# Batches 1 to 7: U, V and z loads issued by ScalarE instead of SyncE, V one step later and split two steps on

## The chip, the cores and the metric

The kernel runs on one core of a Trainium2 chip. The metric is the device time of one execution in microseconds (us). The median of three runs of the kernel before is 2323.25 us (2319.2 to 2325.48).

A core has five engines with their own instruction queues: TensorE (PE, with PEld for its weight loads), VectorE (DVE), ScalarE (ACT), GpSimd (POOL) and SyncE (SP), which does no arithmetic and here only issues DMAs. An engine works its instructions off in order; between engines, semaphores tell what is done.

## The reference, cut to what matters

```python
# u, v: 8 x 2496 x 256, z: 8 x 2496 x 64, fp32
scores = (1.0 / S) * np.matmul(z, z.transpose(0, 2, 1))
attn = np.maximum(scores, 0.0) ** 2
x = u * np.matmul(attn, v)                  # 19968 tokens of 256
# top-1 mixture of 8 experts, 256 -> 1024 -> 256
logits = x @ w_gate
expert_idx = np.argmax(logits, axis=1)      # gate_w: its softmax probability
for e in range(8):
    xe = x[expert_idx == e]
    out[expert_idx == e] = gate_w * (np.maximum(xe @ w1[e], 0.0) @ w2[e])
```

## The kernel before

The first stage, up to about 1345 us of the profile, is the attention. It goes batch by batch (`b`, 8 of them), in each through five chunks of 512 queries (`c`, the last has 448), and in each chunk through ten pairs of key blocks (`kp`): 400 steps, `s` in the loop, with `j` the place in the chunk. The second stage gathers tokens by expert and runs the two expert layers; the change doesn't touch it, except that it follows.

A step does two things on PE. `weighted` multiplies the squared scores of this step with V: 12 matmuls into `acc` (lines 343 to 346). `scores` prepares a later step, three ahead (`LA`): PE multiplies z with z into `ps_s` (lines 306, 307), or turns a block of scores that an earlier chunk stored (line 278), or takes such a block that DMA transposes have turned (line 332, then lines 263 to 265). ACT takes `ps_s` out of PSUM (line 315 with line 316, or line 279), and DVE makes of it a high and a low part, `thi` and `tlo`. `ps_s` has two buffers, so PE can begin the scores of a step only when ACT has emptied the ones of two groups before.

The inputs are loaded in pieces:
- V of a batch in ten pieces of 256 KB, `vr`, with three buffers (`fetch_v`, line 134). `split_v` makes a high part on ACT (line 139) and a low part on DVE (line 140), in `vt`. The V of batch `b + 1` is loaded and split during the last chunk of batch `b`.
- z of a batch in five pieces `zr`, with two buffers (`fetch_z`, line 120), split by `split_z` on ACT (lines 126, 127) and DVE (lines 128, 129), one in each chunk.
- U of a chunk in one piece `u` of 512 KB, with one buffer (`fetch_u`, line 146); `gate_x` multiplies it with the finished `acc` on DVE (line 366) at the chunk's end.

All these loads are issued by SP. SP also issues the DMA transposes of stored scores (line 332, 12 in a batch), those of the chunk's output rows (line 390, four in a chunk, in `turn_rows`; ACT and DVE write their source `th` in lines 385 and 386) and the store of these rows (line 471). As SP works in order, a load is issued behind the transposes that stand ahead of it.

The order on every engine is made by a scheduler from the order in which the code asks for work. Work inside `pinned(...)` is put behind the last instruction that each engine has so far; a load outside of it may be put earlier, as soon as its buffer is free.

Of the kernel before, what the change touches and what calls it, by code (L numbers as in the profile page):

```python
# [47 lines left out]
def fused_kernel(ctx: ExitStack, tc: tile.TileContext, zt, ut, v, wg, wcat, out):  # L48
    nc = tc.nc
# [3 lines left out]
    NKP = NK // 2  # L53
# [55 lines left out]
    zraw, vraw, ztiles, vtiles, utiles = {}, {}, {}, {}, {}  # L109
    zfirst = []  # L110

    def fetch_z(b, c):
        w = P * 4
        if b == 0 and c < 2:
            if c == 0:
                zfirst.append(sb.tile([P, 2, QC], F32, name="x", tag="x"))
            zraw[b, c] = zfirst[0][:, c]
        else:
            zraw[b, c] = sb.tile([P, w], F32, name="zr", tag="zr", bufs=2)
        nc.sync.dma_start(zraw[b, c], zt[b, :, c * w:(c + 1) * w])  # L120

    def split_z(b, c):

# [7 lines left out]

    def fetch_v(b, kp):
        vraw[b, kp] = sb.tile([P, 2, D], F32, name="vr", bufs=3)
        nc.sync.dma_start(vraw[b, kp], v[b, :, 2 * kp:2 * kp + 2, :])

    def split_v(b, kp):
        vr = vraw.pop((b, kp))
# [5 lines left out]
    def fetch_u(b, c):  # L143
        q0, n = chunks[c]
        u = sb.tile([P, 2, QC], F32, name="u")
        nc.sync.dma_start(u[:, :, :n], ut[b, :, :, q0:q0 + n])
        utiles[b, c] = u


# [200 lines left out]
    def pinned(work):  # L350

        last = {}
        for i in nc.cur_bb.bb.instructions[-400:]:
            last[i.engine] = i
        with ExitStack() as behind:
            for i in last.values():
                behind.enter_context(tc.issue_after(i))
            work()
# [489 lines left out]
    plain = [loads[LP - q][-1] for q in range(LP + 1)]  # L848
    for s, (b, c, kp) in enumerate(steps):
        j = s % NKP  # L850
        if j == 2:
            fetch_u(b, c)
        if j == 0:
            accs[b, c] = [ps1.tile([P, QC], F32, name=f"acc{d}", tag="ps1") for d in range(2)]
        if s < NKP:
# [18 lines left out]
        weighted(b, c, kp, j == 0, j == NKP - 1, *ready.pop(s), accs[b, c])  # L874
        if c == NC_ - 1 and b + 1 < B:

            for i in ((0, 1) if j == 0 else (j + 1,) if j < NKP - 1 else ()):
                fetch_v(b + 1, order_of(b + 1, 0)[i])
            if j:
                pinned(lambda: split_v(b + 1, order_of(b + 1, 0)[j - 1]))  # L880
        if c == 0 and j == 0 and b:
            pinned(lambda: split_v(b, order_of(b, 0)[-1]))

        zb, zc = (b + 1, c - 1) if c else (b, NC_ - 1)
        if 0 < zb < B:
            if j == ZF[c > 0]:
                fetch_z(zb, zc)
            if j == ZS[c > 0]:
                pinned(lambda: split_z(zb, zc))

# [112 lines left out]
```

## Time and profile before

| | |
|---|---|
| median of 3 runs | 2323.25 us (2319.2 to 2325.48) |
| the profiled execution | 2324.7 us |
| its span in the trace | 2322.9 us |
| PE busy | 2278.9 us (98%) |
| PEld busy | 1925.6 us (83%) |
| DVE busy | 1632.0 us (70%) |
| ACT busy | 1465.3 us (63%) |
| POOL busy | 625.7 us (27%) |
| loads issued by SP | V 80 x 256 KB, z 40 x 256 KB, U 32 x 512 KB and 8 x 448 KB |

The profile comes from one execution. "Busy" leaves out register, semaphore and DMA-issuing instructions; those stand in the trace under the engine's name with a q (SPq, ACTq). The idle time before an instruction is put down to what released it. A row of the timeline has the start in us, the duration in us, the engine, the line, the operation, what it writes and reads, and in brackets the idle time of the engine before it and its releaser.

### The profile page before, as it was taken

The numbers are of one execution on the slowest core, as the hardware profiler recorded it, in microseconds if no ns is written. First come the engines' busy times: TensorE is split into PE (matmuls) and PEld (weight loads), VectorE is DVE, ScalarE is ACT, GpSimd is POOL, SyncE is SP. The second block draws the span as 40 slices with busy tenths as digits, with TensorE's granted clock in tenths as the row PEclk, the third lists the DMA queues.
The fourth block names the chain that finished last, engine by engine and source line by source line (L and its number), as shares of the span: only waits on it lengthen the run. The fifth ranks groups of instructions, "written<-read, shape, count | busy, mean of one in ns | idle before, by whom it ended". The sixth has DMA issues, their size and how long they took to land.

```text
span 2322.9 us, 33688 instructions
## 1 busy us (share of the span) xinstructions
PE 2278.9 (98%) x12320; PEld 1925.6 (83%) x12320; DVE 1632.0 (70%) x2909; ACT 1465.3 (63%) x1985; POOL 625.7 (27%) x626
## 2 busy tenths in 40 slices
PE   9999999999999999999999989899999999999998
PEld 7888888888888888888888877688888888888887
DVE  8868868878778778877878766455566656657554
ACT  8768668677677777767776654355465555546454
POOL 1011111112102102102111244543445435345322
PEclk9999999999999999999999999899999999999999
DMA  6556656657567367467375484654566646457620
GB/s 163 104 92 135 97 86 135 93 95 134 85 105 132 80 116 121 79 118 125 79 114 95 121 176 89 189 123 131 154 152 173 176 128 207 134 146 194 151 89 29
DMA packets 454366, 287.31 MB, mean 124 GB/s; under 512 B 389100, under 2 KB 411130, under 8 KB 444976
## 3 DMA queue, kind: packets, MB, share of 16 engines
q1 hardware_dynamic: 422800, 165.98, 40.0%
q0 software_dynamic: 31392, 119.10, 17.6%
q8 instruction: 98, 1.61, 0.4%
q14 instruction: 76, 0.62, 0.1%
HBM read 149.79 MB, written 43.43 MB: 83 GB/s over the span
## 4 chain that ended last, share of the span: by engine, by line
PE 85%; issue 4%; DMA 3%; ACT 3%; DVE 2%; POOL 1%; another core or an unknown queue 1%; SPq 0%; POOLq 0%; ACTq 0%
PE ph L776 16%; PE acc L343 13%; PE acc L346 13%; PE acc L345 13%; PE y L799 11%; PE y L802 6%; PE ps_s L306 4%; PE ps_s L307 4%; DMA vr<-in_v_dram 2%; PE ps_s L278 2%; PE pt L398 1%; POOL out_dram L815 1%; PE ps_s L312 1%; DMA rows<-xrows,laidx 1%
## 5 line engine op out<-in xcount | busy, mean ns | idle before, releaser
L346 PE MATMUL acc<-thi,t 128*128 128x512 f32 (+1 forms) x1600 | 614.3, 386 | 0.0
L343 PE MATMUL acc<-thi,t 128*128 128x512 f32 (+1 forms) x1600 | 608.0, 392 | 1.1 <-issue 0.7
L345 PE MATMUL acc<-tlo,t 128*128 128x512 f32 (+1 forms) x1520 | 586.0, 386 | 0.1
L781 DVE SCALAR_TENSOR_TENSOR t<-ph,t 128x512 fp32r<-128x512 f32 (+1 forms) x328 | 220.3, 675 | 238.1 <-ACT t L780 192.5
L776 PE MATMUL ph<-thi,t 128*128 128x512 f32 (+2 forms) x1248 | 379.3, 361 | 3.8 <-issue 2.1
L780 ACT ACTIVATE t<-ph 128x512 fp32r<-128x512 f32 (+1 forms) x328 | 191.9, 591 | 289.1 <-PE ph L776 210.4
L346 PEld LDWEIGHTS acc<-thi,t 128*128 128x128 f32 x1600 | 300.2, 188 | 55.3 <-DVE t L140 0.6
L343 PEld LDWEIGHTS acc<-thi,t 128*128 128x128 f32 x1600 | 299.5, 188 | 54.4 <-DVE x L366 1.2
L345 PEld LDWEIGHTS acc<-tlo,t 128*128 128x128 f32 x1520 | 285.6, 188 | 50.8 <-DVE tlo L319 0.7
L476 POOL DMA_INDIRECT lst<-toks,posi x160 | 197.0, 1231 | 468.2 <-DVE posi L468 425.8
L799 PE MATMUL y<-t,t 128*128 128x512 f32 x1062 | 306.3, 397 | 13.5 <-DVE t L734 6.4
L776 PEld LDWEIGHTS ph<-thi,t 128*128 128x128 f32 x1248 | 226.1, 189 | 32.9 <-issue 2.9
L799 PEld LDWEIGHTS y<-t,t 128*128 128x128 f32 x1062 | 191.5, 191 | 48.7 <-ACT t L780 7.8
L776 PE MATMUL ph<-tlo,t 128*128 128x512 f32 (+2 forms) x624 | 225.6, 362 | 0.7 <-issue 0.7
L815 POOL DMA_INDIRECT out_dram<-tf,lfidx x136 | 143.7, 1057 | 273.4 <-DVE tf L813 245.5
L802 PEld LDWEIGHTS y<-t,t 128*128 128x128 f32 x1062 | 175.8, 190 | 35.2 <-DVE t L781 5.7
L802 PE MATMUL y<-t,t 128*128 128x256 f32 x1062 | 185.0, 283 | 3.6 <-DVE t L781 3.6
L315 ACT ACTIVATE tf<-ps_s 128x1024 f32<-128x1024 f32 (+1 forms) x145 | 133.8, 923 | 85.3 <-PE ps_s L307 43.3
L307 PE MATMUL ps_s<-t,t 128*128 128x512 f32 (+1 forms) x480 | 178.9, 376 | 0.0
L380 POOL MEMSET rows<- 128x64 int32 x40 | 6.8, 172 | 581.7 <-DMA xrows<-rows 359.6
L317 DVE CAST thi<-tf 128x1024 fp32r<-128x1024 f32 (+1 forms) x145 | 90.9, 627 | 102.3 <-ACT tf L316 94.5
L711 POOL DMA_INDIRECT rows<-xrows,lfidx x136 | 138.9, 1021 | 50.2 <-issue 38.3
(252 smaller groups left out, 4050.2 us busy)
## 6 DMA issues: line engine op xcount, KB each, us to landing
vr<-in_v_dram SPq DMA_DIRECT2D x80, 256.0 KB
xrows<-rows SPq DMA_DIRECT2D x32, 544.0 KB
u<-in_ut_dram SPq DMA_DIRECT2D x32, 512.0 KB
zr<-in_zt_dram SPq DMA_DIRECT2D x38, 256.0 KB
u<-in_ut_dram SPq DMA_DIRECT2D x8, 448.0 KB
xrows<-rows SPq DMA_DIRECT2D x8, 408.0 KB
rows<-th SPq DMA_TRANSPOSE x160
lst<-toks,posi POOLq DMA_INDIRECT x160
```

The lines of the kernel that those rows point to most:

```text
L307: nc.tensor.matmul(ps[:, i, m:n], lhsT=hl_k, rhs=lh_q[:, m:n], start=False, stop=True)
L343: nc.tensor.matmul(acc[d][:, :n], lhsT=vh, rhs=hi[:, i, :n], start=first and i == 0, stop=False)
L345: nc.tensor.matmul(acc[d][:, :n], lhsT=vh, rhs=lo[:, i, :n], start=False, stop=False)
L346: nc.tensor.matmul(acc[d][:, :n], lhsT=vl, rhs=hi[:, i, :n], start=False, stop=last and i == 1)
L476: i = nc.gpsimd.indirect_dma_start(out=lst1, out_offset=bass.IndirectOffsetOnAxis(ap=posi[:m, j:j + 1], axis=0), in_=toks[:m, col + j:col ...
L711: nc.gpsimd.indirect_dma_start(out=xg[:, s, :], out_offset=None, in_=src, in_offset=bass.IndirectOffsetOnAxis(ap=lists[which]["idx"][:, s, ...
L776: nc.tensor.matmul(o, lhsT=w1[:, part, dd, fs], rhs=xx[:, dd, :n], start=p == 0, stop=p == 5)
L780: nc.scalar.activation(hh[:, :m], ph[:, :m], AF.Relu)
L781: nc.vector.scalar_tensor_tensor(hl[:, :m], ph[:, :m], 0.0, hh[:, :m].bitcast(F32), op0=ALU.max, op1=ALU.subtract)
L799: nc.tensor.matmul(y, lhsT=h[:, cs], rhs=w2[:, f % 2].rearrange("p i d -> p (i d)"), start=f == 0, stop=False)
L802: nc.tensor.matmul(y[:, 0:D], lhsT=h[:, cs], rhs=w2[:, f % 2, 0, :], start=False, stop=f == NF - 1)
L815: d = nc.gpsimd.indirect_dma_start(out=out, out_offset=bass.IndirectOffsetOnAxis(ap=lists[which]["idx"][:, s, t:t + 1], axis=0), in_=yo[:, ...
```

## The change

For batch 1 and later, the loads of z, V and U are issued by ACT instead of SP: 35 z, 70 V and 35 U loads, 140 of 160. Those of batch 0 stay on SP. All loads of U, of z from batch 1 on and of V from batch 1 on are now pinned, so they are issued at their place in the code and no earlier. U is asked for at step 3 of a chunk instead of step 2. In the last chunk of a batch, piece `j` of the next batch's V is asked for at step `j` (before: pieces 0 and 1 at step 0, piece `j + 1` at step `j`), and piece `j - 2` is split at step `j` (before: `j - 1`); the last two pieces are split in steps 0 and 1 of the next batch.

```diff
--- before.py
+++ after.py
@@ -109,6 +109,9 @@
     zraw, vraw, ztiles, vtiles, utiles = {}, {}, {}, {}, {}
     zfirst = []
 
+    def loads_of(b):
+        return nc.scalar if b else nc.sync
+
     def fetch_z(b, c):
         w = P * 4
         if b == 0 and c < 2:
@@ -117,7 +120,7 @@
             zraw[b, c] = zfirst[0][:, c]
         else:
             zraw[b, c] = sb.tile([P, w], F32, name="zr", tag="zr", bufs=2)
-        nc.sync.dma_start(zraw[b, c], zt[b, :, c * w:(c + 1) * w])
+        loads_of(b).dma_start(zraw[b, c], zt[b, :, c * w:(c + 1) * w])
 
     def split_z(b, c):
 
@@ -131,7 +134,7 @@
 
     def fetch_v(b, kp):
         vraw[b, kp] = sb.tile([P, 2, D], F32, name="vr", bufs=3)
-        nc.sync.dma_start(vraw[b, kp], v[b, :, 2 * kp:2 * kp + 2, :])
+        loads_of(b).dma_start(vraw[b, kp], v[b, :, 2 * kp:2 * kp + 2, :])
 
     def split_v(b, kp):
         vr = vraw.pop((b, kp))
@@ -143,7 +146,7 @@
     def fetch_u(b, c):
         q0, n = chunks[c]
         u = sb.tile([P, 2, QC], F32, name="u")
-        nc.sync.dma_start(u[:, :, :n], ut[b, :, :, q0:q0 + n])
+        loads_of(b).dma_start(u[:, :, :n], ut[b, :, :, q0:q0 + n])
         utiles[b, c] = u
 
 
@@ -848,8 +851,8 @@
     plain = [loads[LP - q][-1] for q in range(LP + 1)]
     for s, (b, c, kp) in enumerate(steps):
         j = s % NKP
-        if j == 2:
-            fetch_u(b, c)
+        if j == 3:
+            pinned(lambda: fetch_u(b, c))
         if j == 0:
             accs[b, c] = [ps1.tile([P, QC], F32, name=f"acc{d}", tag="ps1") for d in range(2)]
         if s < NKP:
@@ -874,17 +877,16 @@
         weighted(b, c, kp, j == 0, j == NKP - 1, *ready.pop(s), accs[b, c])
         if c == NC_ - 1 and b + 1 < B:
 
-            for i in ((0, 1) if j == 0 else (j + 1,) if j < NKP - 1 else ()):
-                fetch_v(b + 1, order_of(b + 1, 0)[i])
-            if j:
-                pinned(lambda: split_v(b + 1, order_of(b + 1, 0)[j - 1]))
-        if c == 0 and j == 0 and b:
-            pinned(lambda: split_v(b, order_of(b, 0)[-1]))
+            if j > 1:
+                pinned(lambda: split_v(b + 1, order_of(b + 1, 0)[j - 2]))
+            pinned(lambda: fetch_v(b + 1, order_of(b + 1, 0)[j]))
+        if c == 0 and j < 2 and b:
+            pinned(lambda: split_v(b, order_of(b, 0)[j - 2]))
 
         zb, zc = (b + 1, c - 1) if c else (b, NC_ - 1)
         if 0 < zb < B:
             if j == ZF[c > 0]:
-                fetch_z(zb, zc)
+                pinned(lambda: fetch_z(zb, zc))
             if j == ZS[c > 0]:
                 pinned(lambda: split_z(zb, zc))
 
```

In the built program, this is what the scheduler makes of it on ACT, at the beginning of the last chunk of batch 0, where the V of batch 1 comes in (`t` is the high part of V, `thi` the high part of scores, `th` the source of the row transposes). Before:

```order
L428 ACTIVATE ex<-dl 128x32
L279 CAST thi<-ps_s 128x2x448 x4
L139 CAST t_1593<-vr 128x512
L279 CAST thi<-ps_s 128x2x448
L139 CAST t_1625<-vr 128x512
L265 CAST thi<-tf 128x2x448
L139 CAST t_1678<-vr 128x512
L385 COPY th<-x 128x1024
L265 CAST thi<-tf 128x2x448
L139 CAST t_1709<-vr 128x512
```

The same place on ACT in the changed kernel, whose line numbers are three higher here (139 has become 142, 279 has become 282, 265 has become 268, 385 has become 388; V is loaded in line 137, z in line 123):

```order
L431 ACTIVATE ex<-dl 128x32
L282 CAST thi<-ps_s 128x2x448 x3
L137 DMA vr<-in_v_dram 128x512
L282 CAST thi<-ps_s 128x2x448
L137 DMA vr<-in_v_dram 128x512
L282 CAST thi<-ps_s 128x2x448
L142 CAST t_1616<-vr 128x512
L137 DMA vr<-in_v_dram 128x512
L123 DMA zr<-in_zt_dram 128x512
L268 CAST thi<-tf 128x2x448
L142 CAST t_1671<-vr 128x512
L268 CAST thi<-tf 128x2x448
```

Each split stands one instruction of score work later, and DMA issues now stand between ACT's instructions.

On SP, in the same chunk and the beginning of the next batch, before:

```order
L146 DMA u<-in_ut_dram 128x2x448
L134 DMA vr<-in_v_dram 128x512 x2
L390 DMA_TRANSPOSE rows<-th 128x4x128 x4
L134 DMA vr<-in_v_dram 128x512 x2
L120 DMA zr<-in_zt_dram 128x512
L134 DMA vr<-in_v_dram 128x512 x3
L332 DMA_TRANSPOSE s_1819<-th 128x16x128
L134 DMA vr<-in_v_dram 128x512
L146 DMA u<-in_ut_dram 128x2x512
L471 DMA xrows<-rows 128x4x272
```

And in the changed kernel (line 390 has become 393, 332 has become 335, 471 has become 474, 146 has become 149):

```order
L149 DMA u<-in_ut_dram 128x2x448
L393 DMA_TRANSPOSE rows<-th 128x4x128 x4
L335 DMA_TRANSPOSE s_1814<-th 128x16x128
L474 DMA xrows<-rows 128x4x272
L335 DMA_TRANSPOSE s_1814<-th 128x16x128
L335 DMA_TRANSPOSE s_1977<-th 128x16x128
```

The V and z loads are gone from between SP's transposes; the U load of batch 0 stays. From here on SP issues transposes and stores only.

## The prediction

> **What bounds the kernel now.** First come the two lines at the head of the page, for the span and the engines; then the table of busy time by stage.
>
> ```profile
> span 2322.9 us, 33688 instructions
> PE 2278.9 (98%) x12320; PEld 1925.6 (83%) x12320; DVE 1632.0 (70%) x2909; ACT 1465.3 (63%) x1985; POOL 625.7 (27%) x626
> ...
> core 0: us, PE busy (x) PEld busy (x) DVE busy (x) ACT busy (x) POOL busy (x), PEclk, DMA share, GB/s
> 0.00:100.00 100.00, 98.60 (x472) 76.84 (x473) 86.30 (x137) 81.63 (x92) 11.74 (x30) 1.00 0.61 140
> 100.00:1340.00 1240.00, 1236.30 (x6779) 1038.18 (x6778) 965.71 (x1680) 874.50 (x1003) 195.31 (x194) 1.00 0.60 107
> 1340.00:1420.00 80.00, 70.56 (x406) 59.09 (x404) 45.44 (x99) 39.34 (x56) 37.26 (x38) 1.00 0.81 158
> 1420.00:2227.00 807.00, 787.33 (x4198) 676.00 (x4197) 489.51 (x919) 429.16 (x762) 364.40 (x349) 0.99 0.58 155
> 2227.00:2322.00 95.00, 86.07 (x473) 75.46 (x471) 45.03 (x76) 40.66 (x75) 17.03 (x18) 0.97 0.10 35
> ```
>
> The reader is to see where PE has idle time at all. The loads that move belong to the stretch from about 100 to 1340 us, and there PE is busy 1236.30 of 1240.00 us: 3.70 us are idle. Busy alone doesn't say that PE runs at its pace, so I looked at single matmuls, in the timeline of PE where the trouble with V is largest.
>
> ```profile
> 850.21 0.36 PE L346 MATMUL acc<-thi,t 128*128 128x448 f32 x1
> ...
> 853.51 0.36 PE L346 MATMUL acc<-thi,t 128*128 128x448 f32 x1
> 854.21 0.50 PE L306 MATMUL ps_s<-t 128*128 128x512 f32 x1 [0.33 <-ACT tf L315]
> ...
> 858.71 0.36 PE L346 MATMUL acc<-thi,t 128*128 128x448 f32 x1
> 858.90 0.48 PE L306 MATMUL ps_s<-t,t 128*128 128x512 f32 x1
> ```
>
> From 850.21 to 853.51 us matmuls follow each other; the starts that the timeline gives are 0.20 us apart for 448 columns, with each lasting 0.36 us, so they overlap. One pause of 0.33 us stands there, and then the score group at 858.90 us starts on time. Next, all that PE waits for between 100 and 1330 us, from the view of the waits:
>
> ```profile
> PE ps_s L306 <- ACT tf L315: 2.8, 4, 1.3
> PE ps_s L278 <- DVE tlo L280: 0.8, 2, 0.7
> ```
>
> Six waits, 3.6 us in all. That is all that a change of loads in this stage can give back. The chain that ended last seems to say otherwise; it has four long pieces of V loads, at four of the seven places where a next batch's V comes in:
>
> ```profile
> 328.31 11.18 DMA vr<-in_v_dram
> 841.22 10.18 DMA vr<-in_v_dram
> 1013.46 10.68 DMA vr<-in_v_dram
> 1184.74 10.12 DMA vr<-in_v_dram
> ```
>
> They come to 42 us, but PE works through them, as its timeline shows; the chain only walks back along what ended last, and the load ended 0.33 us later than PE could hide. The 42 us are not there to be won.
>
> **What the V loads do now.** At one such boundary, ACT and SP:
>
> ```profile
> 845.89 0.95 ACT L316 ACTIVATE tf<-tf 128x896 f32<-128x896 f32 x1
> 851.43 0.62 ACT L139 CAST t<-vr 128x512 fp32r<-128x512 f32 x1 [4.58 <-DMA vr<-in_v_dram]
> ...
> 835.84 0.57 SPq L146 DMA_DIRECT2D u<-in_ut_dram  x1
> 841.22 2.79 SPq L134 DMA_DIRECT2D vr<-in_v_dram  x2
> 844.83 6.45 SPq L390 DMA_TRANSPOSE rows<-th  x4
> ```
>
> The fourth V piece is issued at 841.22 us behind U and lands about 10.2 us later; four row transposes are issued from 3.6 us after it, and their issue ends as it lands. ACT stands still for 4.58 us in front of the split, and PE loses 0.33 us through it. So a stall of 4.58 us on ACT costs PE almost nothing, since scores are three steps ahead.
>
> **The change part by part.** (a) The wait. With V on another queue and both its request and its split a step later, ACT should no longer stand before the fourth split. I take the whole first row of PE's waits as caused by it, since the pause at 854.21 us has this cause in the rows above and there are four of each: −2.8 us. Bounds: 0 (another V piece is late instead) and −3.7 us (all idle time of the stage).
>
> (b) The price on ACT. 140 issues move: 70 of V, 35 of z, 35 of U. No DMA is issued by ACT before, so the nearest rows are those of SP, together with its transposes:
>
> ```profile
> L134 SPq DMA_DIRECT2D vr<-in_v_dram x80: 327/336/1053, 1.3 to 1206.4; - x80
> L120 SPq DMA_DIRECT2D zr<-in_zt_dram x38: 327/714/1256, 2.7 to 1162.3; - x38
> L146 SPq DMA_DIRECT2D u<-in_ut_dram x40: 570/576/1053, 4.6 to 1356.2; - x40
> L332 SPq DMA_TRANSPOSE s<-th x96: 1317/2074/5038, 16.8 to 1333.8; - x96
> L390 SPq DMA_TRANSPOSE rows<-th x160: 1188/1259/9655, 61.9 to 1394.2; - x160
> ```
>
> By the medians: 70 x 0.336 + 35 x 0.714 + 35 x 0.576 = 68.7 us of ACT's sequencer, where ACT has 1240 − 874.5 = 365 us idle. What counts is whether the issue stops ACT's arithmetic. The sequencer runs ahead of it:
>
> ```profile
> L385 ACTq EVENT_SEMAPHORE  x2: 17/28/38, 841.6 to 841.6; - x2
> L385 ACT COPY th<-x x1: 1042/1042/1042, 843.7 to 843.7; 128x1024 uint16<-128x1024 uint16 x1
> ```
>
> ACT's sequencer did the waits of line 385 at 841.6 us, 2.1 us before the copy itself began. An issue of 0.34 us in such a place is covered by what ACT has already queued. I take 0, by these nearest rows. The cover is thinnest from 840 to 875 us, where V is split:
>
> ```profile
> 840.00:875.00 35.00, 34.67 (x192) 29.95 (x190) 28.52 (x51) 28.30 (x36) 0.33 (x2) 1.00 0.79 144
> ```
>
> ACT is busy 28.30 of 35 us; 6.70 us are idle, 4.58 of them the wait above. And PE has some patience: the group at 858.90 us uses the buffer that ACT emptied with this instruction,
>
> ```profile
> 855.55 0.90 ACT L279 CAST thi<-ps_s 128x896 fp32r<-128x896 f32 x1
> ```
>
> ended at 856.45 us, so 2.45 us before PE wanted it. ACT can fall behind by about that much before PE stops. Without cover, the price is the second rival.
>
> (c) A new wait on ACT. A V load needs its buffer free, so it waits for DVE's low part of three pieces before (line 140), and behind it in ACT's queue stand the next emptying of scores and the next split, for which PE and DVE wait. In the timelines of ACT and DVE:
>
> ```profile
> 858.89 0.60 ACT L139 CAST t<-vr 128x512 fp32r<-128x512 f32 x1
> 862.22 0.68 DVE L140 TENSOR_TENSOR t<-vr,t 128x512 fp32r<-128x512 f32 x1
> ```
>
> DVE ended 3.41 us after ACT's cast did. The load that waits for it stands a step later than this split. A step is 3.43 us: a batch has 50, and two V pieces of the chain, at 841.22 and 1013.46 us, are 172.2 us apart. So the wait is over about when it is reached: 0, at most a few tenths, inside the 2.45 us.
>
> (d) U and z elsewhere, one each in a chunk: pinned, with a buffer that DVE has freed by then; ACT has its 365 us. U is asked for a step (3.4 us) later and wanted at the chunk's end, more than six steps on: 0. (e) SP is freed of 140 issues; nothing on PE waits for SP in this stage: 0. (f) In the expert stage only the moment at which it begins changes: 0, either way by what PE idles in the change-over from 1340 to 1420 us, which is the third rival.
>
> Sum: −2.8 us. The profiled execution took 2324.7 us, 1.8 more than its span and 1.45 more than the median; so 2321.9 us as against it, 2320.5 as against the median. I predict **2321 us**: no difference that a measurement can tell, since about 0.3%, or 7 us, is what one of this kernel can separate (2316.3 to 2330.2 us count as the same).
>
> **The rivals.** *It doesn't do what it should: V still comes late.* V goes to another queue, but to the same DMA engines, and in the new order the fourth piece is issued behind U on that queue again. If its 10.18 us stay, against two steps or 6.9 us until the split, ACT waits 3.3 us in place of 4.58, and PE has its 2.8 us of waits or some of them: 2324.7 us. For it speaks that the transposes, which began after the load, ended with it. The Trainium skill has the same, page DMA: Bandwidth & Descriptors, section Issuing engines are not separate DMA queues: all queues end on the same 16 DMA engines, and another issuing engine only saves the time of issuing. By that rule the total would be this rival's; one queue carried both here, so the trace can't yet tell the two apart.
>
> *ACT falls behind (slower).* Every issue shows on ACT and waits for SP's transposes too. In 840 to 875 us there are ten V, two z and two U: 3.4 + 1.4 + 1.2 = 6.0 us. SP's transposes take 96 x 2.07 + 160 x 1.26 = 400 us, 30% of the 1340; an issue that has to wait for one loses half of it, between 0.6 and 1.0 us, say 0.85, so 14 x 0.30 x 0.85 = 3.6 us. Of 9.6 us, ACT takes 6.7 − 4.58 = 2.1 if V still waits, PE's patience 2.45; 5.0 us reach PE, at seven boundaries 35 us: 2360 us. If V's wait is gone, 9.6 against 6.7 + 2.45 leaves 0.4 us a boundary. So it decides from 4.6 us of uncovered issue time per boundary, when V also still waits. Against it: the 2.1 us by which ACT's sequencer was ahead.
>
> The Trainium skill has a rule for this, page Perfetto Trace Analysis, section DMA Instruction — HWDGE (DVE, Sync): the hardware that makes the descriptors is shared by the engines that issue this way and locked for one of them at a time, and the waiting for the lock counts into the instruction. By it, ACT's issue rows would grow whenever SP is in a transpose. With one issuing engine, no row here shows it; without the rule the sum stays as it is.
>
> *The change-over gains (faster).* There SP's queue is slow, and PE pauses:
>
> ```profile
> 1362.44 16.49 SPq L390 DMA_TRANSPOSE rows<-th  x4
> ...
> 1381.73 0.50 PE L776 MATMUL ph<-thi,t 128*128 128x512 f32 x1 [0.97 <-DVE x L366]
> 1389.04 0.74 PE L802 MATMUL y<-t,t 128*128 128x256 f32 x4 [3.37 <-DVE t L781]
> 1401.18 0.40 PE L776 MATMUL ph<-thi,t 128*128 128x512 f32 x1 [1.63 <-issue]
> 1417.96 0.70 PE L799 MATMUL y<-t,t 128*128 128x512 f32 x2 [1.04 <-DVE tf L813]
> ```
>
> Four transposes took 16.49 us there instead of about 5, behind the last U load on SP's queue. If U's leaving shortens that, up to 0.97 + 3.37 + 1.63 + 1.04 = 7.0 us go, and with 3.7 of the attention the time is 2324.7 − 10.7 = 2314.0 us. Against it: gathers fill the same DMA engines then (DMA share 0.81), and U is still among them.
>
> **How the numbers follow.** My forecast 0.50; V still late 0.16; ACT behind 0.23; the change-over 0.11. The first two lie within 0.3%: same 0.66, slower 0.23, faster 0.11. The range goes from 2313 us (the third rival and a margin of 1) to 2342 us, half of the slower rival's 35 us above 2324.7; beyond it I leave what is left of that rival.
>
> **What would show it.** (a) right: no ACT wait for V at line 139's split above 1 us, and PE's first row of waits under 1 us; wrong: 3 us at another V piece. (b) right: ACTq rows near SP's medians and ACT's idle time before its next instruction unchanged; wrong: rows of 1 us and more, and PE waiting for line 315 or 279 between V splits. (c) wrong: ACTq issues held by line 140. If PE's idle time from 100 to 1340 us is over 10 us, the forecast is wrong in the place of the second rival; if it is under 4 and the time still moves by more than 7 us, the change-over or the expert stage did it, which I hold at 0.

## The result, and the profile after

The changed kernel takes 2353.44 us (median of 6 runs, 2345.03 to 2362.01) against 2323.64 us (median of 6 runs) for the kernel before: a ratio of 1.0129, 95% interval 1.0107 to 1.0151. It is 30 us slower; the prediction was 2321 us, in a range that ended at 2342 us. The profiled execution took 2351.25 us.

The head of the page, and the table of busy time by stage, of the changed kernel:

```profile
span 2349.5 us, 33649 instructions
PE 2289.4 (97%) x12320; PEld 1931.1 (82%) x12320; DVE 1634.1 (70%) x2909; ACT 1465.6 (62%) x1985; POOL 628.5 (27%) x626
```

```profile
100.00:1340.00 1240.00, 1221.27 (x6651) 1023.16 (x6650) 952.53 (x1654) 862.15 (x988) 190.67 (x185) 1.00 0.63 105
1340.00:1420.00 80.00, 71.30 (x413) 60.27 (x412) 48.01 (x89) 42.31 (x53) 28.31 (x29) 0.96 0.85 158
```

In the stretch from 100 to 1340 us PE was idle 3.70 us before; now it is 1240 − 1221.27 = 18.73 us. The last matmul into `acc` starts at 1408.4 us in place of 1378.1 us, so the attention carries the whole 30 us; the stage behind it takes no longer than before (from the first `ph` matmul to the end of the span 940.9 us, before 944.5).

The view of the waits (what waited, for what: us in total, times, longest). First the row of the kernel before for V, from 100 to 1340 us; then the changed kernel, four rows from 100 to 1340 us and the last one from 1340 to 1420 us:

```profile
ACT t L139 <- DMA vr<-in_v_dram: 27.7, 10, 5.6
```

```profile
ACT t L142 <- DMA vr<-in_v_dram: 40.0, 16, 6.4
ACT t L129 <- DMA zr<-in_zt_dram: 13.8, 8, 3.0
PE ps_s L281 <- ACT tf L318: 9.4, 4, 3.3
PE ps_s L309 <- ACT tf L318: 6.3, 4, 3.1
...
PE acc L346 <- ACT thi L282: 5.4, 1, 5.4
```

ACT's waits for V have not gone; they grew from 27.7 us (10 times) to 40.0 us (16 times), waits for z have come in, and PE, which lost 2.8 us to ACT, now loses 15.7 us there and 5.4 us more in the last chunk.

Which pieces of V are late is read at one boundary, from batch 3 to batch 4, in the timeline of the changed kernel (start, duration, engine, line; the idle time before it and its releaser in brackets):

```profile
678.14 0.96 POOL L479 DMA_INDIRECT lst<-toks,posi  x1 [26.67 <-DVE posi L471]
679.40 0.96 POOL L479 DMA_INDIRECT lst<-toks,posi  x1 [0.30 <-issue]
680.66 1.47 POOL L479 DMA_INDIRECT lst<-toks,posi  x1 [0.30 <-DMA xrows<-rows]
681.11 0.33 ACTq L137 DMA_DIRECT2D vr<-in_v_dram  x1
682.44 0.96 POOL L479 DMA_INDIRECT lst<-toks,posi  x1 [0.31 <-issue]
682.82 0.33 ACTq L137 DMA_DIRECT2D vr<-in_v_dram  x1
...
692.65 0.62 ACT L142 CAST t<-vr 128x512 fp32r<-128x512 f32 x1 [6.42 <-DMA vr<-in_v_dram]
693.03 1.11 ACTq L123 DMA_DIRECT2D zr<-in_zt_dram  x1
694.23 0.55 ACTq L149 DMA_DIRECT2D u<-in_ut_dram  x1
694.87 0.94 ACT L268 CAST thi<-tf 128x896 fp32r<-128x896 f32 x1 [1.61 <-DVE lw L405]
...
697.18 0.91 ACT L318 ACTIVATE tf<-ps_s 128x896 f32<-128x896 f32 x1
...
698.14 1.97 PE L281 MATMUL ps_s<-ident,s 128*128 128x128 f32 x8 [3.28 <-ACT tf L318]
```

The reader is to see that it is pieces 0 and 1 now, not the fourth. They are asked for at 681.11 and 682.82 us, in the midst of four scatters by which POOL writes token numbers into the list of an earlier chunk, 4 bytes each (`lst`, line 479). ACT reaches the split and stands 6.42 us; behind the split in its queue stands the emptying of `ps_s` (line 318), so PE runs out of scores and stands 3.28 us. Part of that is a second delay: behind the split ACT issues z and U, and the conversion of line 268 starts 0.09 us after the second issue ends, 1.61 us late. (The view names a reduction on DVE, but that had ended at 694.16 us.) In v_only, a run below in which ACT issues neither z nor U, the same conversion follows its split at this boundary without a pause:

```profile
688.90 0.62 ACT L142 CAST t<-vr 128x512 fp32r<-128x512 f32 x1 [7.05 <-DMA vr<-in_v_dram]
...
689.43 0.94 ACT L268 CAST thi<-tf 128x896 fp32r<-128x896 f32 x1
```

In the kernel before, the timeline of the boundary from batch 4 to 5 has these pieces far ahead:

```profile
695.62 3.45 SPq L134 DMA_DIRECT2D vr<-in_v_dram  x2
703.60 0.45 SPq L134 DMA_DIRECT2D vr<-in_v_dram  x1
...
838.21 0.96 POOL L476 DMA_INDIRECT lst<-toks,posi  x1 [0.30 <-issue]
...
839.37 0.63 ACT L139 CAST t<-vr 128x512 fp32r<-128x512 f32 x1
841.84 0.62 ACT L139 CAST t<-vr 128x512 fp32r<-128x512 f32 x1
843.20 0.61 ACT L139 CAST t<-vr 128x512 fp32r<-128x512 f32 x1
```

Pieces 0 to 2 of batch 5 were issued at 695 to 704 us, as soon as their three buffers were free, some 140 us ahead of their splits, and no split waited. Only the fourth piece, asked for at 841.22 us just behind the last scatter (838.21 us), was long there too.

The pauses cost PE twice. The table of busy time for four short stretches of the changed kernel, each behind a pause; the third number from the end is the granted TensorE clock:

```profile
350.00:353.40 3.40, 3.12 (x8) 2.62 (x9) 2.15 (x5) 2.63 (x5) 0.00 (x0) 0.51 1.23 209
524.00:527.40 3.40, 3.40 (x11) 3.04 (x10) 3.33 (x5) 3.32 (x6) 0.00 (x0) 0.50 1.09 161
698.10:701.50 3.40, 3.36 (x13) 3.19 (x14) 2.40 (x5) 3.33 (x5) 0.20 (x1) 0.50 1.10 344
1374.00:1380.80 6.80, 5.88 (x22) 5.14 (x23) 6.21 (x14) 2.31 (x4) 3.65 (x3) 0.50 0.79 248
```

For 17 us the clock is at half, which is worth at most 8.5 us of work; the attention before has no such stretch. So 15.0 us more idle time of PE up to 1340 us, 4.7 us more in the last chunk (6.4 in place of 1.6) and 8.5 us of clock make 28.2 of the 30.2 us.

### The profile page after: what moved, and what is told of

It is laid out like the page before. It is cut to its first block, busy times and chain, and to the rows that moved or that the text cites. A ratio compares the mean times of both kernels' runs of the same rounds, so it can differ in the third digit from the quotient of the medians.

```text
span 2349.5 us, 33649 instructions
## 1 busy us (share of the span) xinstructions
PE 2289.4 (97%) x12320; PEld 1931.1 (82%) x12320; DVE 1634.1 (70%) x2909; ACT 1465.6 (62%) x1985; POOL 628.5 (27%) x626
## 3 DMA queue, kind: packets, MB, share of 16 engines
q8 instruction: 98, 1.61, 0.4%
## 4 chain that ended last, share of the span: by engine, by line
PE 78%; DMA 8%; issue 5%; ACT 4%; DVE 3%; POOL 1%; another core or an unknown queue 1%; SPq 0%; ACTq 0%; POOLq 0%; DVEq 0%
PE ph L779 17%; PE acc L346 12%; PE acc L349 12%; PE y L802 11%; PE acc L348 11%; PE y L805 6%; PE ps_s L309 4%; DMA zr<-in_zt_dram 4%; PE ps_s L310 4%; DMA vr<-in_v_dram 3%; PE ps_s L281 1%; DMA s<-th 1%; PE pt L401 1%; ACT tf L318 1%
## 5 line engine op out<-in xcount | busy, mean ns | idle before, releaser
L479 POOL DMA_INDIRECT lst<-toks,posi x160 | 202.1, 1263 | 526.7 <-DVE posi L471 486.2
L318 ACT ACTIVATE tf<-ps_s 128x1024 f32<-128x1024 f32 (+1 forms) x145 | 133.5, 921 | 78.6 <-PE ps_s L310 41.4
L269 DVE TENSOR_TENSOR tlo<-tf,thi 128x1024 fp32r<-128x1024 f32 (+1 forms) x96 | 115.3, 1201 | 52.7 <-ACT thi L268 49.9
```

Of the source, the lines that this page charges most:

```text
L318: nc.scalar.activation(a[:, :, m:n], ps[:, :, m:n], AF.Relu)
L479: i = nc.gpsimd.indirect_dma_start(out=lst1, out_offset=bass.IndirectOffsetOnAxis(ap=posi[:m, j:j + 1], axis=0), in_=toks[:m, col + j:col ...
```

## The experiments

All times are ratios to the kernel before, run beside it. The first theory, A: V pieces 0 to 2 have lost their lead and now are loaded where loads are slow; ACT, in order, stands at the split, and PE behind it. B is the prediction's second rival, that ACT pays for the issues. C: the pinned places or the later split as such. `V waits` are the waits of ACT's splits for V from 100 to 1340 us, `PE idle` is 1240 us less PE's busy time there, and `attention` is how much later than in the kernel before (1378.1 us) the last matmul into `acc` starts. The three come from one profiled execution each.

| kernel | ratio (95%) | V waits, us | PE idle, us | attention, us |
|---|---|---|---|---|
| changed kernel | 1.0129 (1.0107 to 1.0151) | 40.0 | 18.7 | +30.2 |
| issue_price | 1.0025 (1.0008 to 1.0042) | 28.7 | 3.8 | +1.3 |
| v_early | 1.0123 (1.0091 to 1.0155) | 3.1 | 10.3 | +21.5 |
| scat_early | 1.0157 (1.0095 to 1.0219) | 53.6 | 10.2 | +47.1 |
| v_as_before | 1.0047 (1.0027 to 1.0067) | 32.8 | 6.1 | +10.2 |
| v_early0 | 1.0048 (1.0027 to 1.0068) | 2.5 | 7.6 | +21.3 |
| all_on_sp | 1.0022 (1.0002 to 1.0042) | 40.8 | 8.9 | +10.2 |
| engine_only | 1.0049 (1.0032 to 1.0066) | 24.6 | 12.8 | +14.5 |
| u_as_before | 1.0125 (1.0089 to 1.0162) | 51.2 | 24.9 | +31.1 |
| scat_late | 1.0141 (1.0098 to 1.0183) | 4.5 | 25.2 | +39.9 |
| v_early0_u | 1.0015 (0.9997 to 1.0034) | none | 2.3 | −1.4 |
| v_only | 1.0083 (1.0056 to 1.0111) | 50.9 | 19.6 | +22.5 |
| v_only_early0 | 0.9981 (0.9964 to 0.9998) | 12.0 | 1.0 | −3.1 |
| before_scat_late | 1.0255 (1.0238 to 1.0273) | 9.4 | 41.4 | +56.1 |

The ratio holds the second stage as well, which no edit here touches. In these profiles it took 933 to 951 us (944.5 in the kernel before), but for before_scat_late, which ran on a faster chip; why it varies isn't known. The last column is steadier: four kernels that were profiled twice differ in it by 1 to 5 us. Where ratio and column disagree, the column is the better sign of what the loads did.

Three numbers for each V load are worked out from the traces: its lead (from issue to split), the time from its issue to its last packet, and ACT's idle time just before the split. For batches 1 to 7, the medians (idle time: mean):

| kernel | piece 0: lead, load, idle | piece 1: lead, load, idle | piece 3: lead, load, idle |
|---|---|---|---|
| before | 143.0, 3.8, 0 | 142.4, 2.4, 0 | 10.1, 6.4, 3.5 |
| changed | 8.7, 7.9, 3.9 | 11.3, 10.3, 0.9 | 7.6, 5.9, 0 |
| v_early | 30.9, 6.5, 0 | 26.8, 4.2, 0 | 8.1, 7.7, 0.1 |
| v_early0 | 125.4, 5.3, 0 | 121.2, 3.7, 0 | 10.8, 9.8, 0.1 |
| all_on_sp | 9.4, 3.4, 0 | 10.7, 4.9, 0.2 | 9.3, 7.5, 2.0 |
| engine_only | 142.1, 3.3, 0 | 141.3, 2.3, 0.3 | 8.6, 6.3, 3.5 |
| scat_late | 5.0, 2.3, 0.5 | 4.9, 2.3, 0.2 | 6.7, 3.1, 0 |
| v_only | 10.4, 8.2, 5.8 | 12.2, 8.7, 1.3 | 6.9, 2.9, 0 |

### The price of the issues (issue_price)

```diff
+    def ping(b):
+        if b:
+            d = sb.tile([P, 4], F32, name="dm", bufs=8)
+            nc.scalar.dma_start(d[0:1], zt[b, 0:1, 0:4])
...
+        if j == 3:
+            pinned(lambda: ping(b))
...
+            pinned(lambda: ping(b + 1))
...
                 fetch_z(zb, zc)
+                pinned(lambda: ping(zb))
```

> The kernel before, with all loads left where they were, and 140 further DMAs of 16 bytes that ACT issues at the places where the changed kernel issues U, V and z (nothing reads them). Theory A (lead): the loss comes from V pieces 0 to 2 being asked for only some 7 us ahead of their split, not from issuing on ACT: the ratio to the kernel before lies within 0.997 and 1.003, PE's idle time from 100 to 1340 us stays under 6 us. Theory B (price of the issues on ACT, the recorded second rival): 20 to 30 us longer, ratio 1.009 to 1.013.

Measured: 1.0025. The added issues and the stretch of the attention, in the line view and in the table of busy time:

```profile
L115 ACTq DMA_DIRECT2D dm<-in_zt_dram x140: 208/209/757, 58.4 to 1360.0; - x140
```

```profile
100.00:1340.00 1240.00, 1236.25 (x6776) 1037.45 (x6775) 964.93 (x1678) 872.91 (x1004) 178.16 (x193) 1.00 0.59 106
```

140 issues of 209 ns leave PE's idle time at 3.75 us. By its interval the kernel is 2 to 10 us slower, so not quite nothing, but at most a third of the loss. The changed kernel's own V issues take 334 ns at the median and 506 at most:

```profile
L137 ACTq DMA_DIRECT2D vr<-in_v_dram x70: 334/334/506, 155.0 to 1233.7; - x70
```

Theory B is out as the main cause, but its mechanism is there in part. From 100 to 1340 us of the changed kernel ACT's arithmetic stands idle 14 times until an issue of its own ends, as at 694.87 us above; the issues fill 10.7 us of these pauses, 2.4 us in the longest. issue_price has no such pause, but its issues are shorter and nothing in it makes ACT wait for V first. v_only, below, has 1.7 us of such time in place of 10.7, and PE's idle time is as long.

### Thirty microseconds of lead (v_early)

```diff
-            pinned(lambda: fetch_v(b + 1, order_of(b + 1, 0)[j]))
+            if j > 2:
+                pinned(lambda: fetch_v(b + 1, order_of(b + 1, 0)[j]))
+        if c == NC_ - 2 and 4 <= j <= 6 and b + 1 < B:
+            pinned(lambda: fetch_v(b + 1, order_of(b + 1, 0)[j - 4]))
```

> The changed kernel, with the first three V pieces of a next batch asked for in steps 4 to 6 of the chunk before the last (about 30 us ahead of their split in place of 7), still by ACT and pinned; the number of issues on ACT and the splits stay. Theory A: the waits of ACT for V fall from 40 us to under 20, PE's idle time at the seven boundaries goes, what stays is the last chunk of batch 7 (about 7 to 10 us): 2328 to 2338 us, ratio 1.002 to 1.006. Theory B: nothing changes, 2350 us and more, ratio 1.011 to 1.015.

Measured: 1.0123, a miss in the time. The waits for V went (3.1 us), as theory A says, but others came. The view of the waits of v_early from 100 to 1340 us, and its timeline in the chunk before the last of batch 4:

```profile
ACT tf L266 <- DMA s<-th: 23.3, 7, 5.1
ACT t L129 <- DMA zr<-in_zt_dram: 18.4, 12, 3.7
...
ACT t L142 <- DMA vr<-in_v_dram: 3.1, 7, 1.2
```

```profile
822.89 8.40 SPq L335 DMA_TRANSPOSE s<-th  x2
...
823.75 0.34 ACTq L137 DMA_DIRECT2D vr<-in_v_dram  x1
827.75 0.33 ACTq L137 DMA_DIRECT2D vr<-in_v_dram  x1
...
834.23 1.36 ACT L266 COPY tf<-s 128x1024 uint16<-128x1024 uint16 x1 [5.05 <-DMA s<-th]
```

At the new place V meets the two score transposes whose result ACT needs first in the next chunk; they take 8.40 us, ACT stands 5.05 us in front of line 266, and PE pauses 2.76 us at 837 us. The V lead isn't enough; what else is under way at the time counts. In the profile the attention ends 21.5 us late in place of 30.2, and the second stage takes 950.6 us, which hides that gain in the total. The theory was mended: a load that ACT issues at its place meets other DMAs, and whichever of them has the nearest deadline stops ACT.

### Over a hundred microseconds of lead (v_early0)

The same edit with `if c == (b == 0) and 5 <= j <= 7` and piece `j - 5`: pieces 0 to 2 come in the batch's first chunk, in batch 0 in its second.

> The changed kernel, with the first three V pieces of a next batch asked for in steps 5 to 7 of the batch's first chunk (of its second in batch 0), by ACT and pinned; more than 100 us ahead of their split, as the kernel before had them, and away from the score transposes whose result is wanted at the beginning of the last chunk. Theory A, mended (crowding: a load that ACT issues at its place meets other DMAs on the same engines, and whichever of them has the nearest deadline stalls ACT; asked for 30 us ahead V met the score transposes of the chunk before the last): ACT waits for V under 10 us and no score transpose there takes over 4 us, so what stays is z and the last chunk of batch 7: 2330 to 2341 us, ratio 1.003 to 1.008. Theory C (the lead of V isn't the cause, pinning or the later split is): 2345 us and more, ratio over 1.010.

Measured: 1.0048, inside, though partly by luck: the attention ends 21.3 us late, no earlier than in v_early, and the second stage took 933.0 us in place of 950.6. What bears on theory A is the stretch up to 1340 us: V no longer stops ACT (2.5 us), no score transpose is waited for longer than 2.0 us, and PE idles 7.6 us in place of v_early's 10.3. The last chunk, in turn, has become slower. What stays, in the view of the waits (the first row from 100 to 1340 us, the others from 1335 to 1385 us):

```profile
ACT t L129 <- DMA zr<-in_zt_dram: 28.1, 13, 4.0
...
ACT tf L266 <- DMA s<-th: 15.0, 1, 15.0
PE acc L346 <- ACT thi L282: 11.3, 1, 11.3
```

### V alone, and all but V (v_only, v_as_before, v_only_early0)

v_only is the kernel before with only the V part of the change; v_as_before is the changed kernel with only that part put back; v_only_early0 is v_only with the edit of v_early0.

> The kernel before with the V part of the change alone: ACT, pinned, split two steps on; z and U as before on SP. Theory A: pieces 0 to 2 are asked for 6 to 12 us ahead, the boundaries cost 15 to 25 us, the last chunk of batch 7 nothing: 2335 to 2348 us, ratio 1.006 to 1.011. If V's new place costs only together with z and U on the same queue: 2328 us and less, ratio under 1.004.

> The changed kernel with V alone put back: SP, unpinned, split one step on. z and U stay on ACT, pinned, U at step 3. Theory A: the seven boundaries are as in the kernel before, the last chunk of batch 7 keeps its loss and ACT waits some us for z: 2326 to 2338 us, ratio 1.001 to 1.006. Theory B: half of the 140 issues stay, so half of the loss: 2338 to 2342 us, ratio about 1.0065.

> The V part of the change alone with its lead given back: ACT, pinned, split two steps on, pieces 0 to 2 asked for in steps 5 to 7 of the batch's first chunk; z and U as before on SP. It is what the prediction took the change to be. Theory A: no boundary loses, ACT waits for V under 5 us, PE idles under 6 us from 100 to 1340 us: 2315 to 2324 us, ratio 0.997 to 1.001. If the issues on ACT or the later split cost something of their own: ratio 1.003 and more.

Measured: 1.0083, 1.0047 and 0.9981, each inside theory A's range of times; only the waits of ACT for V in v_only_early0 are longer than expected (12.0 us, the longest 3.2), and PE hides them. V's part is worth 0.0083 x 2323 = 19 us, that of z and U 11 us, each within about 6 us; in the attention they are 22.5 and 10.2 us. Together they make about the 30 us. v_as_before alone doesn't tell A from B, whose 1.0065 lies within its interval; the other two do, since both have all 70 V issues on ACT. With its lead given back, V's part is no loss any more: the 24 us between v_only and v_only_early0 are the price of loading pieces 0 to 2 at the boundary. The stretch of the attention in the two, first v_only, then v_only_early0:

```profile
100.00:1340.00 1240.00, 1220.39 (x6659) 1023.57 (x6658) 952.59 (x1656) 861.20 (x990) 190.34 (x187) 1.00 0.60 105
```

```profile
100.00:1340.00 1240.00, 1239.01 (x6807) 1042.56 (x6806) 967.19 (x1680) 876.77 (x1006) 201.69 (x197) 1.00 0.64 107
```

PE is idle 19.61 us in the one and 0.99 us in the other.

### Queue without places, places without queue (engine_only, all_on_sp)

engine_only has `loads_of` in the kernel before and nothing else; all_on_sp is the changed kernel with `return nc.sync` in `loads_of`.

> The kernel before, with nothing changed but the engine that issues the loads of batches 1 to 7: ACT in place of SP, unpinned, at the old places, split one step on. Theory A: on ACT's queue a load cannot run ahead of the score work in front of it, so pieces 0 and 1 are asked for one step ahead and not over 100 us: as slow as the changed kernel or slower, 2345 to 2375 us, ratio 1.009 to 1.022. Theory C (the places): 2318 to 2332 us, ratio 0.998 to 1.004.

> The changed kernel, with all loads issued by SP again, at the changed kernel's places in the code, pinned, V split two steps on. SP's order has V pieces 0 to 2 right behind the store of the chunk before, before U. Theory A (crowding and lead by way of ACT's queue): SP is free to issue them as soon as it gets there, one queue carries loads and transposes one after the other: 2320 to 2334 us, ratio 0.999 to 1.005. Theory C (the places): as slow as the changed kernel, ratio over 1.010. Theory B would also say 1.000.

all_on_sp measured 1.0022, inside. Its V loads have a lead of only 9 to 13 us, but SP issues them at 664.45 us at the boundary shown above, 0.1 us ahead of the first scatter, and they take 3.4 to 5.8 us. engine_only measured 1.0049, a miss for both theories: my premise was wrong, since unpinned loads keep their lead on ACT's queue too (142 us in the table). Its loss has another form: ACT waits for DVE (9.5 us for line 436, 6.3 us for line 143, 4.6 us for line 405) with the split one step behind, and the score transposes from 100 to 1400 us take 3.02 us at the median in place of 2.06. So neither half of the change makes the whole loss; it takes the pinned places on a queue that does arithmetic. But neither half is free, as the totals seem to say: in both kernels the last `acc` matmul ends 10 to 14 us later than before, and a second stage that is 8 us shorter hides most of it. Why it is shorter, these runs don't show.

### U alone put back (u_as_before, v_early0_u)

```diff
-        if j == 3:
-            pinned(lambda: fetch_u(b, c))
+        if j == 2:
+            fetch_u(b, c)
...
-        loads_of(b).dma_start(u[:, :, :n], ut[b, :, :, q0:q0 + n])
+        nc.sync.dma_start(u[:, :, :n], ut[b, :, :, q0:q0 + n])
```

u_as_before is the changed kernel with this, v_early0_u is v_early0 with this.

> The changed kernel, with U alone put back: SP, unpinned, step 2. V and z stay on ACT, pinned. Theory A: z no longer has U right behind it on its queue, and in the last chunk of batch 7 U is asked for ahead of the scatters again, so the pause of 5.4 us near 1369 us goes: 2338 to 2347 us, ratio 1.006 to 1.010, the loss at the boundaries stays. If U has no part: 2350 us and more.

> The kernel v_early0 (V pieces 0 to 2 over 90 us ahead, by ACT) with U put back to SP, unpinned, step 2. z stays on ACT, pinned. With V early there is no V load for U to meet, so what putting U back does for the last chunk of batch 7 (the pause of 11 us there and the clock at half for 13.7 us behind it) should show this time: 2320 to 2328 us, ratio 1.000 to 1.003. If the rest of the loss is z's: ratio 1.004 and more, ACT's waits for z as in v_early0 (28 us).

u_as_before measured 1.0125, a miss. In the last chunk of batch 7 the pause went, as expected: no pause there is over 0.7 us. But SP now issues U at 326.87 us at the first boundary, 2 us ahead of V's pieces 0 and 1; piece 0 is waited for 10.62 us there and PE pauses 7.74 us. What U gave at one place it took at another. v_early0_u, in which no V load stands there, measured 1.0015, inside: putting U back is worth 7.7 us then by the ratios, with 1 to 14 us left open by their intervals, and 22.7 us in the attention of the two profiles. Why U costs in the last chunk is seen in the timeline of the changed kernel:

```profile
1343.93 1.06 POOL L479 DMA_INDIRECT lst<-toks,posi  x1 [0.30 <-issue]
...
1344.23 0.55 ACTq L149 DMA_DIRECT2D u<-in_ut_dram  x1
...
1349.00 8.11 SPq L393 DMA_TRANSPOSE rows<-th  x4
1357.22 7.77 SPq L335 DMA_TRANSPOSE s<-th  x2
...
1368.84 1.33 ACT L266 COPY tf<-s 128x1024 uint16<-128x1024 uint16 x1 [9.04 <-DMA s<-th]
```

U's 512 KB stand behind the scatters, the transposes behind them take 8.11 and 7.77 us, ACT waits 9.04 us and PE 5.4 us. Before, U went out at 1313.92 us, ahead of them. In v_early0_u only z is left beside the V part. ACT's waits for z (32.3 us) are as long as in v_early0, but PE's idle time is 2.34 us, and the attention ends 1.7 us later than in v_only_early0. In the total z's cost stays open: the intervals of v_early0_u and v_only_early0 overlap.

### Are the scatters the cause? (scat_early, scat_late, before_scat_late)

In scat_early the parts of the routing follow each other with two steps less between them (`[nothing] * 2` becomes `[nothing] * 0`).

> The changed kernel, with the routing of a chunk (choose, exps, place) two steps earlier, so that POOL's four scatters of the token list run about 7 us earlier and no longer while V pieces 0 and 1 are under way. If the loads are long because they meet the scatters (theory A with this cause): V pieces 0 and 1 take 2 to 4 us instead of 9 to 12, ACT's waits for V fall below 25 us, 2330 to 2342 us, ratio 1.003 to 1.008. If they are long for another reason (their own queue, the transposes), nothing changes: ratio 1.011 to 1.015, and the same under theory B.

Measured: 1.0157, and it tells nothing about the cause: V's issue moved with the scatters. At the boundary into batch 3 the scatters begin at 498.78 us and V is asked for at 502.33 us, 3.5 us behind, as in the changed kernel (503.57 and 506.84). A large part of its loss is of another kind, a single wait of PE for DVE of 18.4 us in the last chunk. The next edit holds them back by what they wait for:

```diff
-            posi = sb.tile([P, ns], I32, name="posi", bufs=2)
-            nc.vector.tensor_copy(posi, posr)
...
-            for j in range(ns):
...
+            def scatter():
+                posi = sb.tile([P, ns], I32, name="posi", bufs=2)
+                nc.vector.tensor_copy(posi, posr)
+                for j in range(ns):
...
+            if t0 < (B - 2) * S:
+                kept.append(scatter)
+            else:
+                scatter()
...
+        if c < NC_ - 1 and j == 5:
+            while kept:
+                pinned(kept.pop(0))
```

> The changed kernel, with the last step of the routing (the cast of the positions on DVE and POOL's four scatters of the token list) kept back, for batches 0 to 5, until step 5 of the next chunk that is no last chunk; the store of the rows by SP stays where it is. It tells two causes of the long loads apart. If the scatters make them long: V pieces 0 and 1 take 2 to 5 us in place of 8 to 10 at the boundaries into batches 1 to 6, ACT's waits for V fall below 20 us, what stays is the boundary into batch 7 and the last chunk: 2328 to 2340 us, ratio 1.004 to 1.009. If the store of 544 KB just ahead of them does it, or the V loads among themselves: the loads stay at 8 to 10 us, ratio 1.010 to 1.015.

Measured: 1.0141, a miss in the time, but the loads answer the question. Pieces 0 and 1 land 2.3 us after their issue in place of 7.9 and 10.3, with the store of 544 KB still 5 us ahead of them, and the waits of ACT's splits for V fall to 4.5 us, 2 times (7.6 us more are put down to V in front of line 268). At the one boundary whose scatters stayed, into batch 7, they take 8.1 and 10.0 us as ever. A lead of 5 us is enough when no scatter runs. The table of busy time while V comes in at the boundary into batch 3, first of the changed kernel, then of scat_late (the last two numbers are the busy share of the 16 DMA engines, and GB/s):

```profile
507.00:518.00 11.00, 11.00 (x76) 10.00 (x76) 4.19 (x4) 2.55 (x4) 1.70 (x3) 1.00 0.68 42
```

```profile
511.00:522.00 11.00, 11.00 (x77) 10.09 (x76) 7.41 (x10) 8.48 (x12) 0.25 (x2) 1.00 0.68 187
```

The DMA engines are as busy in both, and move 42 GB/s in the one and 187 in the other. (The rate alone would say little, since seven loads are issued in the second stretch, and in the first only two are under way, with a third at its end.) Where the time of scat_late goes: eight scatters are issued together from 389 us on, among score transposes,

```profile
388.67 13.81 SPq L335 DMA_TRANSPOSE s<-th  x2
...
404.58 18.97 SPq L335 DMA_TRANSPOSE s<-th  x1
```

of which one takes 18.97 us (in the changed kernel 5.85 at most). The last packet of these scatters in the trace starts at 401.5 us, so the long transpose comes behind them and not beside them; by what means they would delay it isn't shown. That they do is read from the edit: the longest score transpose takes 17 to 21 us in each of the four runs with kept-back scatters. To see what is left of the change then, the kernel before got the same edit:

> The kernel before, with the cast of the positions and the four scatters kept back for batches 0 to 5 exactly as in scat_late; loads as before. If the scatters at V's place are what makes the change slow, they now cost both kernels the same: 2345 to 2358 us, ratio 1.009 to 1.014, so that the change itself is worth under 0.4% on top of it, with waits of ACT for the score transposes of 30 us and more as in scat_late. If the changed places of the loads cost something that doesn't come from the scatters, this kernel stays under 1.006 and scat_late lies 0.8% and more above it.

It measured 1.0255, a miss for both of its ranges, but on a chip on which the kernel before takes 2288.81 us, so it doesn't compare with scat_late. Four kernels were run once more on one chip:

> scat_late again, beside before_scat_late_2 on the same chip. If the loss of the change comes from its loads meeting the scatters, scat_late_2 is no slower than before_scat_late_2: its time over that one's between 0.985 and 1.002. If the places cost something of their own, over 1.006.

> before_scat_late again, beside scat_late_2 on the same chip: the kernel before with the scatters kept back loses 1.0 to 2.6% through its score transposes. Against scat_late_2 as said there.

> The changed kernel itself on the same chip as the others of this set: ratio to the kernel before 1.010 to 1.016, as first measured; on a chip on which the second stage is faster the same 28 to 34 us, ratio 1.012 to 1.017.

> v_only_early0 again, the V part of the change with its lead given back: 2.7 us less idle time of PE in the attention by its first trace, so a ratio of 0.996 to 1.000. If the first 0.998 was chance, 1.000 to 1.003.

| kernel | median, us | ratio (95%) |
|---|---|---|
| scat_late_2 | 2363.82 | 1.0164 (1.0143 to 1.0186) |
| before_scat_late_2 | 2378.64 | 1.0233 (1.0211 to 1.0255) |
| after_2 | 2352.91 | 1.0141 (1.0095 to 1.0186) |
| v_only_early0_2 | 2318.28 | 0.9978 (0.9963 to 0.9993) |

All four are inside. With the scatters moved, the change is no loss but a gain: 2363.82 over 2378.64 is 0.994. The same loads at the same places on the same engine cost 1.3 to 1.4% beside the scatters and nothing away from them; but both kernels idle PE for 28 to 40 us elsewhere then, which may hide a small cost.

The clearest sign is the fourth V piece in before_scat_late_2, which goes by SP's queue in the kernel before's order. At the six boundaries without scatters it lands 2.2 to 3.3 us after its issue (in the kernel before 3.2 to 10.1), and its split never waits. At the seventh, whose scatters stayed, it takes 8.2 us and the split waits 4.4 us. The four row transposes follow it by 3.6 to 4.8 us at all seven.

And V's part with its lead is faster than the kernel before, by 0.2%, in both of its runs.

## Why the prediction was wrong, point by point

**The bound** held: what PE waits for sets this stage, and no row put the 3.7 us of idle time higher.

**Step (a) failed.** It took the wait of ACT for V to go: −2.8 us, with bounds of 0, "another V piece is late instead", and −3.7. For the fourth piece it was right, whose split waited 3.5 us before and now waits for nothing (means of seven boundaries). But the section on what the V loads do now looked at the fourth piece alone. Pieces 0 to 2 had a lead of about 140 us because they weren't pinned; the change takes it away, which the diff and the order of ACT showed, and the step had no term for it. Its bound of 0 assumed that PE can hide any late piece as it hid a wait of 4.58 us at 851.43 us. The sign that the prediction had set for this, 3 us at another V piece, came: 3.9 us at piece 0. Behind a wait of 6.42 us PE stood 3.28 us, and the clock was at half for 3.4 us after it. Measured: +19 us for V's part with the late pieces, −4 to −5 us (0.9981 and 0.9978) with their lead given back. So −2.8 us was the right size for what the step spoke of: PE's idle time went from 3.70 to 0.99 us in v_only_early0.

**Step (b)**, no price for 140 issues on ACT, was nearly right as long as ACT has work queued: V's issues take 334 ns, and 140 further ones left PE's idle time at 3.75 us and the time 2 to 10 us longer. It failed where nothing is queued that could cover an issue, behind a late split above all: 10.7 us of ACT's pauses, and at the boundary shown up to 1.6 us of PE's 3.28. How much of the 30 us that makes, no run separates.

**Step (c)** was right: with two steps to the split no V issue waited for DVE in the changed kernel. engine_only, with one step, has waits of ACT for DVE of 20 us, which fits; but its loads aren't pinned either, so that the later split is what keeps the waits away isn't shown. (A step is 172.2 / 50 = 3.44 us, not the 3.43 of that paragraph; nothing hangs on it.)

**Step (d) failed too**: U and z at 0. It counted whether they come in time and not what is under way at their new places; they cost 11 us by v_as_before. U's share, 7.7 us once V is out of the way, looks like the larger one, though its interval is wide.

**Step (e)**: SP's freedom gave nothing that shows; its score transposes take 2.04 us at the median, before 2.07. **Step (f)**: the second stage differs by 3.6 us of 944, with the sign of the third rival, but it varies by more than that between runs; no run was made on it.

**The first rival** (V still late) named the right kind of cause, for the wrong pieces and at too small a price. Its witness was the wrong one as well: the fourth piece was long in the kernel before because it was issued 3 us behind the scatters, not because of the four row transposes, as before_scat_late_2 shows. The Trainium skill's rule that it leaned on, page DMA: Bandwidth & Descriptors, section Issuing engines are not separate DMA queues, holds as far as it goes: another queue didn't keep V away from the other DMAs.

**The second rival** came out near the size (35 us against 30) by luck: of its mechanism only the small part happened that step (b) tells, and the prediction's last paragraph would have booked 18.7 us of idle time to it. issue_price and v_only_early0 are what keeps the two apart. No wait for a shared lock is seen: 13 of V's issues on ACT begin while SP is in a transpose, and they take 334 to 393 ns. Single issues of z and U were longer (1.1 and 3.0 us), but none of them began in a transpose.

What stays open: z's own share of the total, why the second stage is 8 us shorter in all_on_sp and engine_only and varies as it does, and why the change gains 15 us once the scatters are moved.

## What to carry to other kernels

Before a load is pinned, or given to an engine that does arithmetic, measure its lead from issue to first use, for every piece and not only for the one that waits today: an unpinned load may be far ahead without showing in any wait. At its new place, look at which other DMAs are under way, and what is queued behind the instruction that waits for it. A place without neighbours is worth as much as a long lead: 5 us were enough in one kernel, 10 us were too few in another.

## What the runs showed of the hardware

Four scatters of 128 numbers, 4 bytes each, slow the loads that are issued behind them: 256 KB issued 3 to 5 us after the first scatter take 8 to 10 us in place of 2.3, while in all_on_sp the piece issued 0.1 us ahead of it took 3.4. The slow loads run at the same busy share of the DMA engines (0.68) and a quarter of the rate (42 against 187 GB/s). The Trainium skill, page DMA: Bandwidth & Descriptors, section Specifications, says that a transfer under 512 bytes is made by reading, changing and writing back; that would fit, and no run here shows it.

A pause of PE of 2.49 us (at 520.3 us) or 3.28 us (at 694.9 us) was followed by 3.4 us at half the clock; pauses of 1.3 us weren't. The length alone doesn't decide it: a pause of 1.52 us at 1797.9 us of the changed kernel was followed by such a stretch, and the one of 3.37 us that ends at 1389.04 us in the kernel before was not. The Trainium skill, page TensorE: Matmul & The Clock Gate, section HAM oscillation — how this bites in real kernels, puts the limit at gaps of about 3.4 us; here shorter ones were enough at some places.

On one chip the kernel before took 2288.81 us, on the others 2320 to 2325 us. The difference lies in the second stage: in before_scat_late it took 909 us there, in the same kernel as before_scat_late_2 on another chip 941 us, while the attention ended at 1435 us on both. What differs between the chips isn't known.
